# Two weight conversions on ScalarE ordered behind named exps of the attention, in a fused attention and mixture-of-experts kernel

## The chip, the cores and the metric

The kernel runs on one core of one Trainium2 chip. The metric is the device time of one execution in microseconds (us). The engines are called PE (TensorE, matrix products), DVE (VectorE), ACT (ScalarE), POOL (GpSimd) and SP (SyncE, which here only issues transfers). PEld is PE's loading of the stationary operand.

## What is computed

Three stages follow each other. Clustered attention over 2 x 8 heads of 768 rows of 64: a query sees only the keys whose nearest of 16 centroids is its own. Then a layer of 8 experts (512 to 1024 to 512), where each of the 1536 rows goes to the one expert with the largest gate value. Then a dense layer (512 to 2048 to 512) with the activation h * tanh(softplus(h)).

```python
def reference(**kwargs):
    attn_out = _attn_ref(q, k, v, centroids)     # softmax over the keys of the same cluster
    x = attn_out.transpose(0, 2, 1, 3).reshape(B * S, H * D)
    x = _moe_ref(x, modality_id, w_gate, modality_bias, w1, w2)
    return _moe2_ref(x, w_in, w_out)
# _moe_ref, for each expert e:
    h = np.maximum(x[mask] @ w1[e], 0.0)
    out[mask] = gate_w[mask, None] * (h @ w2[e])
```

## The kernel before, in words

All products are made of float16 pairs: a float32 value is split into a high half (hi) and the rest (lo), and a product is the sum of three matmuls, hi*hi, hi*lo and lo*hi.

*Attention* walks over 16 heads with 6 key tiles of 128 each. `st_step` (L382) makes the scores of one key tile in two halves of 384 columns (PE, L391) and their exps (ACT, L393) into the float32 tile `e32` (called `ef` where the exp is used unsplit). `e_hi` (L396) copies it to the hi half `eh` (ACT, L400), `e_low` (L402) makes the lo half `el` on POOL by subtraction (L114), and `av_step` multiplies with the values (L425 to L429). Beside this run, for later heads: `split_pair` (the split `hl` of a pair of heads, L245 on ACT, L249 on POOL), `stack` (SP copies `hl` into the operand tile `QK`, L258 to L261), `assign` (the cluster of each row, ending in a copy `oT` on ACT, L301, that SP loads into `QK`, L303), and `smax` (the row maxima, PE L350 and L355, DVE L351 and L356).

*The gate and the sorting.* When the eight heads of the first batch are done, `gate` ranks its 768 rows by expert and POOL scatters them to DRAM in that order (tensor `dr`, L822). SP brings them back as `xs` (L853), ACT makes a diagonal matrix of each row's gate value (`diag`, tile `dg`, L707), and PE transposes and scales the rows with it (L718) to the sorted block `xw`, which ACT (L722) and DVE (L725) split again.

*The experts.* `moe1` (L948) takes the two experts of a batch with the most rows. It streams their weights in chunks of 512 KB through three helpers: `w_load` (L917) issues the load into the float32 tile `wf`, which has two buffers; `w_hi` (L936) makes the hi half on ACT (L939), `w_lo` (L942) the lo half on DVE (L943), both into tile `w`, which has three buffers. For the first batch the loads are issued by ACT (`WQ = 2`), behind the lo half of the chunk that held the buffer. The first two chunks are loaded and converted ahead of the loop in `moe1`, chunk n + 2 while chunk n is multiplied. The products start when the block `xw` is whole (L1028, read by ACT at L986).

*The dense layer's weights* are turned from float64 to float16 pairs in the meantime: `convs` loads 16 chunks of w_in (tile `raw`, SP, L1040), which DVE shifts and joins (L1048 to L1051, L1056) and ACT copies (L1054).

*Order of the work.* The Python code interleaves these generators; a scheduler then sets the order of the instructions of each engine, except that of SP, which stays as written. An engine takes its instructions in that order, and a waiting instruction holds up all behind it. `moe1` is started when the first weights' loads are issued, while the attention of the second batch goes on:

```python
    wq = []
    for k_ in range(2):
        wq.append(w_hi(wf_t[order[k_]]))
        yield 0.5
        w_lo(wf_t[order[k_]], wq[-1])
        if k_ == 0:
            w_load(*order[2])
        yield 0.5
```

Of the kernel before, what the change touches and what calls it, by code (L numbers as in the profile page):

```python
# [13 lines left out]
AF = mybir.ActivationFunctionType  # L14
# [10 lines left out]
def clustered_attention_moe_kernel(  # L25
# [16 lines left out]
    nc = tc.nc  # L42
    B, H, D, S = qT.shape
# [6 lines left out]
    HS = S // 2  # L50
# [25 lines left out]
    F32T = (2, 5)  # L76
    F32H = 16
    WL = 0
    FAST = 1
    CI1 = 2  # L80
    CQ = 0
# [28 lines left out]
    def eps(shape, dt=F32):  # L110
        return ps_e.tile(shape, dt, tag="e", name="eps")
# [266 lines left out]
        nc.scalar.activation(out=QK[i % NST][96:98, QB, :], in_=pt[96:98, 0:S], func=AF.Copy)  # L378

    e_t = {}  # L380

    def st_step(i, kt):  # L382
        st = QK[i % NST]
        full = i < F32H and kt in F32T
        e32 = a3.tile([P, S], F32, tag="e32", name="ef" if full else "e32", bufs=4)
        eh = None if full else a3.tile([P, S], F16, tag="eh", name="eh", bufs=3)
        el = None if full else a3.tile([P, S], F16, tag="el", name="el", bufs=3)
        sps = [eps([P, 512]) if i < SE and (2 * (T * i + kt) + hf) % SM == SM - 1 else ps_s.tile([P, 512], F32, tag="s", name="s") for hf in range(2)]
        for hf in range(2):
            for a in range(2):  # L390
                nc.tensor.matmul(sps[hf][:, 0:HS], lhsT=st[:, KA + a, kt * P:(kt + 1) * P], rhs=st[:, QA + a, hf * HS:(hf + 1) * HS], start=(a == 0), stop=(a == 1))  # L391
        for hf in range(2):
            nc.scalar.activation(out=e32[:, hf * HS:(hf + 1) * HS], in_=sps[hf][:, 0:HS], func=AF.Exp, scale=1.0 / float(D) ** 0.5)  # L393
        e_t[i, kt] = (eh, el, e32)

    def e_hi(i, kt):  # L396
# [34 lines left out]
    def fin(i):  # L431

        b, h = divmod(i, H)
        av = av_t.pop(i)
        if h == 0:
            xb[b] = l2.tile([P, T, ROW], F16, tag="xb", name="xb")
        x = xb[b]
        r = sm.tile([P, T, 1], F32, tag="r", name="r")
        xt = sm.tile([P, T, D], F32, tag="xt", name="xt", bufs=1)
        nc.vector.tensor_scalar(out=r, in0=av[:, :, D:], scalar1=32.0 / 256, scalar2=32e-9 / 256, op0=ALU.mult, op1=ALU.add)  # L440
        nc.vector.reciprocal(out=r, in_=r)
        nc.vector.tensor_tensor(out=xt, in0=av[:, :, 0:D], in1=r.to_broadcast([P, T, D]), op=ALU.mult)  # L442
        yield 3
        hi = x[:, :, h * D:(h + 1) * D]
        nc.scalar.activation(out=hi, in_=xt, func=AF.Copy)
        yield 2
        (nc.vector if FLD and h == H - 1 else nc.gpsimd).tensor_tensor(out=x[:, :, DM + h * D:DM + (h + 1) * D], in0=xt, in1=hi, op=ALU.subtract)
        fin_done.add(i)
        yield
# [44 lines left out]
    def attention():  # L494
# [28 lines left out]
        def run(g):  # L523
            for _ in g:
                pass
# [10 lines left out]
        def av_next():  # L536

            k = 1 + (len(avq) > AVL)
            while avq and k:
# [9 lines left out]
                if j == 1 and kt == T - 1:  # L549
                    gap[0] = GAP  # L550
                    if i % H == H - 1 and FAST:
                        run(fin(i))
# [57 lines left out]
        for n in range(N + LAG):  # L610
            i, kt = divmod(n, T)
            i_, k_ = divmod(n - LAG, T)
            if n < N:
                if kt == 0:
                    if i + 3 < NH:
                        stack(i + 3)
                    if i == 1:
                        put(gate_consts())
                    if i % H == H - 4 and i < NH - H:
                        load_v(i // H + 1, 0, T)  # L620
                if i % 2 == 1 and kt in (1, 2) and i + 5 < NH:
                    load_pair((i + 5) // 2, kt - 1)
                p_ = i // 2 + 2
                if 2 * p_ < NH:
                    if i % 2 == 0 and kt in (SPK, SPK + 1):
                        run(split_pair(p_, kt - SPK, False, kt - SPK < HLD))
                st_step(i, kt)
# [287 lines left out]
    wf_t = {}  # L915

    def w_load(b, s, n):  # L917

        eng = nc.scalar if WQ and (b, s) == (0, 0) and n < 2 or WQ > 1 and b < WQ - 1 else nc.sync
        if (b, s, eng) not in reg_t:  # L920
            reg_t[b, s, eng] = eng.value_load(reg_t[b][0:1, s:s + 1], min_val=0, max_val=E - 1)
        wf_t[b, s, n] = w_dma(reg_t[b, s, eng], n, eng)
# [13 lines left out]
    def w_hi(f):  # L936
        shp = f.shape
        hl_ = wts.tile([shp[0], 2, shp[1], shp[2]], F16, tag="w", name="w")
        nc.scalar.activation(out=hl_[:, 0], in_=f, func=AF.Copy, scale=32.0)  # L939
        return hl_  # L940

    def w_lo(f, hl_):  # L942
        nc.vector.scalar_tensor_tensor(out=hl_[:, 1], in0=f, scalar=32.0, in1=hl_[:, 0], op0=ALU.mult, op1=ALU.subtract)  # L943
# [4 lines left out]
    def moe1():  # L948

        order = [(b, s, n) for b in range(B) for s in range(2) for n in range(8)]  # L950
# [4 lines left out]
        yield 0.5  # L955
        wq = []
        for k_ in range(2):
            wq.append(w_hi(wf_t[order[k_]]))
            yield 0.5
            w_lo(wf_t[order[k_]], wq[-1])  # L960
            if k_ == 0:
                w_load(*order[2])
            yield 0.5
# [334 lines left out]
    m_p["raw"] = ctx.enter_context(tc.tile_pool(name="raw", bufs=RAWB))  # L1298
    gs0, gs1 = Stepper(lambda: gate(0)), Stepper(lambda: gate(1))
    M = moe1()  # L1300
    CI = convs("i")
    m_done = [0.0]
# [12 lines left out]
    for na, _ in enumerate(attention()):  # L1315
# [6 lines left out]
        if 0 in reg_t and (0, 0, 0) not in wf_t:  # L1322
            wl += 1
            if wl > WL:
                w_load(0, 0, 0)
# [67 lines left out]
```

## Time and profile before

| | us |
|---|---|
| three runs | 675.71, 677.24, 678.28 |
| median | 677.24 |
| profiled execution | 677.5 |
| its span, first to last instruction | 675.8 |

Busy in that span: PE 617.2 us (91%), ACT 455.1 (67%), DVE 375.9 (56%), POOL 256.3 (38%). Attention takes the time to about 300 us, the experts overlap it from 200 on, and the dense layer fills the rest. The shares are averages over stages with different limits, so a change in one stage is read from that stage's own rows. Times in the rows are counted from the span's start; a row gives the start, the duration, and in brackets the idle time of that engine just before it with what ended it.

### The profile page before, as it was taken

The numbers are of one execution on the slowest core, as the hardware profiler recorded it, in microseconds if no ns is written. First come the engines' busy times: TensorE is split into PE (matmuls) and PEld (weight loads), VectorE is DVE, ScalarE is ACT, GpSimd is POOL, SyncE is SP. The second block draws the span as 40 slices with busy tenths as digits, with TensorE's granted clock in tenths as the row PEclk, the third lists the DMA queues.
The fourth block names the chain that finished last, engine by engine and source line by source line (L and its number), as shares of the span: only waits on it lengthen the run. The fifth ranks groups of instructions, "written<-read, shape, count | busy, mean of one in ns | idle before, by whom it ended". The sixth has DMA issues, their size and how long they took to land. (4 is left out here: it accounts for less than half of the span.)

```text
span 675.8 us, 13675 instructions
## 1 busy us (share of the span) xinstructions
PE 617.2 (91%) x5474; PEld 421.9 (62%) x5475; DVE 375.9 (56%) x745; ACT 455.1 (67%) x704; POOL 256.3 (38%) x229
## 2 busy tenths in 40 slices
PE   1789989989698997989999899999999999999995
PEld 1467768858476765656775567566666667666442
DVE  5757666787689899998568898522311101101000
ACT  4578798877697767565887776656655676767300
POOL 5457775887764435220521211111311222223111
PEclk9789999999799999999999999999999999999998
DMA  7632353312971443463454555221000000000000
GB/s 219 156 74 72 90 161 100 94 42 66 274 239 37 135 129 117 144 205 98 168 164 169 157 156 186 63 63 32 32 1 1 17 17 1 31 1 16 17 32 35
DMA packets 56742, 64.42 MB, mean 95 GB/s; under 512 B 10080, under 2 KB 46944, under 8 KB 56672
## 3 DMA queue, kind: packets, MB, share of 16 engines
q1 hardware_dynamic: 42064, 48.74, 25.1%
q10 hardware_dynamic: 12688, 8.42, 4.3%
q0 software_dynamic: 1920, 6.32, 2.5%
q8 instruction: 45, 0.74, 0.5%
q14 instruction: 25, 0.20, 0.1%
HBM read 46.23 MB, written 6.32 MB: 78 GB/s over the span
## 5 line engine op out<-in xcount | busy, mean ns | idle before, releaser
L114 POOL TENSOR_TENSOR el<-e,eh 128x768 f16<-128x768 f32 x64 | 109.0, 1707 | 79.8 <-ACT eh L400 47.8
L1028 PE MATMUL h<-x,win 128*128 128x256 f16 x1152 | 131.8, 273 | 0.2 <-POOL x L1015 0.2
L1028 PEld LDWEIGHTS <-win 128*128 128x128 f16 x1152 | 112.6, 98 | 19.0 <-issue 0.4
L1028 PEld LDWEIGHTS <-w 128*128 128x128 f16 x768 | 74.4, 98 | 66.8 <-issue 11.1
L1133 DVE SCALAR_TENSOR_TENSOR s<-s,h 128x512 f32<-128x512 f32 x48 | 30.8, 684 | 149.0 <-ACT s L1129 149.0
L1184 PE MATMUL o<-wout,xb 128*128 128x512 f16 x432 | 95.9, 379 | 0.0
L114 POOL TENSOR_TENSOR xb<-s,xb 128x1024 f16<-128x1024 f32 x18 | 40.2, 2232 | 134.1 <-ACT xb L1136 134.1
L391 PE MATMUL s<-QK 128*128 128x384 f16 x320 | 78.2, 334 | 7.7 <-ACT e L393 5.9
L1028 PE MATMUL eps<-xw,w 128*128 128x416 f16 x384 | 72.8, 339 | 8.1 <-DVE hT L990 2.9
L351 DVE TENSOR_REDUCE mxh<-x 128x1 f32<-128x512 f32 x96 | 64.7, 681 | 16.3 <-PE x L350 15.8
L1028 PE MATMUL eps<-hT,w 128*128 128x416 f16 x384 | 71.8, 339 | 1.6 <-DVE hT L990 1.6
L1184 PEld LDWEIGHTS <-xb 128*128 128x128 f16 x432 | 42.3, 98 | 48.3
L393 ACT ACTIVATE e<-s 128x384 f32<-128x384 f32 x112 | 52.7, 491 | 22.2 <-PE s L391 18.0
L400 ACT ACTIVATE eh<-e 128x768 f16<-128x768 f32 x64 | 54.2, 849 | 0.7
L391 PEld LDWEIGHTS <-QK 128*128 128x128 f16 x384 | 34.5, 103 | 24.8 <-issue 13.0
L425 PE MATMUL av<-vst,ef 128*128 128x65 f32 x384 | 49.9, 272 | 0.0
L425 PEld LDWEIGHTS av<-vst,ef 128*128 128x128 f32 x384 | 48.5, 191 | 1.9
L427 PE MATMUL av<-vst,eh 128*128 128x65 f16 x384 | 45.4, 193 | 3.1 <-DVE xt L442 2.6
L1127 ACT ACTIVATE s<-h,cst 128x512 f32<-128x512 f32 x48 | 33.0, 688 | 21.7 <-PE h L1028 21.4
L428 PE MATMUL av<-vst,eh 128*128 128x64 f16 x384 | 45.6, 195 | 0.0
L943 DVE SCALAR_TENSOR_TENSOR w<-wf,w 128x1024 f16<-128x1024 f32 x32 | 42.7, 1334 | 4.4 <-ACT w L939 4.3
L429 PE MATMUL av<-vst,el 128*128 128x65 f16 x384 | 43.6, 192 | 0.9 <-POOL el L114 0.8
(245 smaller groups left out, 1090.8 us busy)
## 6 DMA issues: line engine op xcount, KB each, us to landing
wf<-in_moe_w_dram ACTq DMA_DIRECT2D x16, 512.0 KB
raw<-in_moe_w_in_dram SPq DMA_DIRECT2D x16, 512.0 KB
raw<-in_moe_w_out_dram SPq DMA_DIRECT2D x16, 512.0 KB
wf<-in_moe_w_dram SPq DMA_DIRECT2D x16, 512.0 KB
QK<-hl SPq DMA_DIRECT2D x32, 192.0 KB
xs<-dr SPq DMA_DIRECT2D x12, 258.0 KB
t<-in_k_dram SPq DMA_DIRECT2D x8, 384.0 KB
t<-in_q_dram SPq DMA_DIRECT2D x8, 384.0 KB
```

Source lines behind the costliest of these rows:

```text
L114: nc.gpsimd.tensor_tensor(out=out_, in0=in0, in1=in1, op=ALU.subtract)
L351: nc.vector.reduce_max(out=mx_t[i][:, t, 0:1], in_=sp, axis=AX.X)
L391: nc.tensor.matmul(sps[hf][:, 0:HS], lhsT=st[:, KA + a, kt * P:(kt + 1) * P], rhs=st[:, QA + a, hf * HS:(hf + 1) * HS], start=(a == 0), st ...
L393: nc.scalar.activation(out=e32[:, hf * HS:(hf + 1) * HS], in_=sps[hf][:, 0:HS], func=AF.Exp, scale=1.0 / float(D) ** 0.5)
L400: nc.scalar.activation(out=eh, in_=e32, func=AF.Copy)
L425: nc.tensor.matmul(av[:, t, :], lhsT=e32[:, cols], rhs=vs[:, h, :], start=(kt == 0 and t == 0), stop=(kt == T - 1), skip_group_check=True)
L427: nc.tensor.matmul(av[:, t, :], lhsT=eh[:, cols], rhs=vs[:, h, 0:NV], start=(kt == 0 and t == 0), stop=False, skip_group_check=True)
L428: nc.tensor.matmul(av[:, t, 0:D], lhsT=eh[:, cols], rhs=vs[:, h, NV:], start=False, stop=False, skip_group_check=True)
L429: nc.tensor.matmul(av[:, t, :], lhsT=el[:, cols], rhs=vs[:, h, 0:NV], start=False, stop=(kt == T - 1), skip_group_check=True)
L943: nc.vector.scalar_tensor_tensor(out=hl_[:, 1], in0=f, scalar=32.0, in1=hl_[:, 0], op0=ALU.mult, op1=ALU.subtract)
L1028: nc.tensor.matmul(out_, lhsT=wc[:, a, kk, ms], rhs=mv[:, c, kk, :], start=(i == 0), stop=(i == n - 1))
L1184: nc.tensor.matmul(pts[t], lhsT=gsl[q % 2][f // FB][:, f % FB, a, t * P:(t + 1) * P], rhs=wout[:, c, f, :], start=(f == 0 and i_ == 0), st ...
```

## The change

Each exp of the attention is now noted in a list, `e_ins`. The hi half of each of the first two weight chunks is made inside `tc.issue_after(...)` of the twelfth last exp noted so far (`EW = 12`): the scheduler may place the conversion on ACT only behind that exp. Both are ACT's own instructions, so this sets their order and adds no instruction. By the buffer numbers the first conversion (tile `w_3903`) is tied to the first exp of tile `e32_3502`, the second (`w_3951`) to the first exp of `e32_3568`.

```diff
+    EW = 12
...
     e_t = {}
+    e_ins = []
...
         for hf in range(2):
-            nc.scalar.activation(out=e32[:, hf * HS:(hf + 1) * HS], in_=sps[hf][:, 0:HS], func=AF.Exp, scale=1.0 / float(D) ** 0.5)
+            ei_ = nc.scalar.activation(out=e32[:, hf * HS:(hf + 1) * HS], in_=sps[hf][:, 0:HS], func=AF.Exp, scale=1.0 / float(D) ** 0.5)
+            e_ins.append(ei_)
...
         for k_ in range(2):
-            wq.append(w_hi(wf_t[order[k_]]))
+            with tc.issue_after(e_ins[-EW].ins):
+                wq.append(w_hi(wf_t[order[k_]]))
```

The new lines shift the numbers behind them: L393, L400, L707, L722, L933 and L939 of before are L395, L403, L710, L725, L936 and L942 of the change.

The order of ACT's instructions behind the first two weight loads, before. `w` is the converted chunk, `wf` the loaded one, `s` a half of the scores; the rows with DMA issue loads:

```order
L939 ACTIVATE w_3903<-wf_2832 128x1024
L301 ACTIVATE oT_3176<-oC_3314 128x384
L393 ACTIVATE e32_3237<-s_3240 128x384
L939 ACTIVATE w_3951<-wf_2834 128x1024
L393 ACTIVATE e32_3237<-s_3241 128x384
L393 ACTIVATE e32_3276<-s_3279 128x384
L933 ISA
L933 DMA wf_3929<-in_moe_w1_dram 128x4x256
L400 ACTIVATE eh_3238<-e32_3237 128x768
L393 ACTIVATE e32_3276<-s_3280 128x384
L393 ACTIVATE ef_3318<-s_3319 128x384
L400 ACTIVATE eh_3277<-e32_3276 128x768
```

The same place on ACT with the change:

```order
L302 ACTIVATE oT_3176<-oC_3314 128x384
L395 ACTIVATE e32_3237<-s_3240 128x384
L395 ACTIVATE e32_3237<-s_3241 128x384
L403 ACTIVATE eh_3238<-e32_3237 128x768
L395 ACTIVATE e32_3276<-s_3279 128x384
L395 ACTIVATE e32_3276<-s_3280 128x384
L403 ACTIVATE eh_3277<-e32_3276 128x768
L395 ACTIVATE ef_3318<-s_3319 128x384
L395 ACTIVATE ef_3318<-s_3320 128x384
L246 ACTIVATE hl_3273<-t32_3018 128x768
```

Both conversions and the third load are gone from here; exps, their hi halves and the split of the next pair follow each other.

The place on ACT where the two conversions and the third load now stand, with the change; `dg` are the diagonal matrices, `xw` the copies of the sorted block:

```order
L710 ACTIVATE dg_3618<-ident16_103,xs_3482 128x128 x2
L395 ACTIVATE e32_3502<-s_3505 128x384
L942 ACTIVATE w_3903<-wf_2832 128x1024
L302 ACTIVATE oT_3433<-oC_3633 128x384
L725 ACTIVATE xw_3535<-eps_3585 128x4x128
L710 ACTIVATE dg_3668<-ident16_103,xs_3482 128x128 x2
L395 ACTIVATE e32_3502<-s_3506 128x384
L395 ACTIVATE e32_3568<-s_3571 128x384
L942 ACTIVATE w_3951<-wf_2834 128x1024
L403 ACTIVATE eh_3503<-e32_3502 128x768
L936 ISA
L936 DMA wf_3929<-in_moe_w1_dram 128x4x256
```

Before, the conversions of three chunks and the issue of the third to fifth load stood ahead of the first `dg` row; with the change all of these stand behind it, and the conversion of the first chunk comes behind that of the third `dg`.

## Rows read from the trace of the kernel before

**Rows 1.** The cores: span and mean granted clock of PE.

```profile
core 0: 675.8 us, clock 0.985
```

**Rows 2.** Busy us by stretch: its length, PE, PEld, DVE, ACT, POOL, clock, DMA.

```profile
185.00:205.00 20.00, 19.46 (x279) 15.63 (x276) 17.37 (x37) 19.65 (x46) 12.64 (x10) 1.00 0.70 217
...
190.00:220.00 30.00, 26.41 (x334) 20.07 (x333) 27.51 (x57) 25.50 (x57) 16.37 (x14) 1.00 0.39 107
220.00:260.00 40.00, 37.90 (x397) 26.34 (x395) 37.22 (x62) 28.57 (x51) 14.95 (x11) 1.00 0.46 137
260.00:320.00 60.00, 54.95 (x505) 36.71 (x505) 54.37 (x88) 37.26 (x66) 16.48 (x10) 1.00 0.47 141
...
440.00:640.00 200.00, 200.00 (x1319) 128.78 (x1317) 33.19 (x50) 124.81 (x137) 44.32 (x28) 1.00 0.06 19
```

**Rows 3.** The timeline of ACT (ACTq: its issuing of loads), 167 to 180.

```profile
167.89 1.01 ACTq L933 DMA_DIRECT2D wf<-in_moe_w_dram  x2
...
171.62 1.06 ACT L939 ACTIVATE w<-wf 128x1024 f16<-128x1024 f32 x1
172.56 0.85 ACT L301 ACTIVATE oT<-oC 128x384 f16<-128x384 f16 x1
...
178.39 1.06 ACT L939 ACTIVATE w<-wf 128x1024 f16<-128x1024 f32 x1 [4.59 <-issue]
178.68 0.42 ACTq L933 DMA_DIRECT2D wf<-in_moe_w_dram  x1
```

**Rows 4.** The timeline of PE, 172 to 181.

```profile
172.99 0.49 PE L391 MATMUL s<-QK 128*128 128x384 f16 x2
...
174.93 0.49 PE L391 MATMUL s<-QK 128*128 128x384 f16 x2
179.88 1.44 PE L391 MATMUL s<-QK 128*128 128x384 f16 x4 [4.47 <-ACT e L393]
```

**Rows 5.** Busy time by stretch again, around PE's gap.

```profile
177.00:180.00 3.00, 0.12 (x1) 0.10 (x1) 1.23 (x3) 1.61 (x3) 0.93 (x1) 0.52 1.05 399
180.00:184.00 4.00, 4.00 (x32) 2.33 (x30) 3.03 (x6) 3.91 (x7) 2.86 (x2) 0.50 0.79 225
```

**Rows 6.** The timeline of POOL: the lo halves behind the last scatter.

```profile
181.03 3.40 POOL L114 TENSOR_TENSOR el<-e,eh 128x768 f16<-128x768 f32 x2 [3.10 <-ACT eh L400]
```

**Rows 7.** The timeline of SP's issues, 178 to 188.

```profile
178.39 1.23 SPq L303 DMA_DIRECT2D QK<-oT  x2
...
184.04 2.71 SPq L853 DMA_DIRECT2D xs<-dr  x6
```

**Rows 8.** Packets, MB, share by queue in 174-180; 180-184 (two); 184-186; 186-191.

```profile
q1 hardware_dynamic: 523, 0.63, 43.6%
...
q10 hardware_dynamic: 507, 0.50, 40.6%
q0 software_dynamic: 105, 0.32, 31.0%
...
q10 hardware_dynamic: 410, 0.42, 67.4%
...
q1 hardware_dynamic: 859, 1.58, 90.7%
```

**Rows 9.** The timeline of DVE, 173 to 202.

```profile
173.97 0.69 DVE L356 TENSOR_REDUCE mxh<-x 128x2 f32<-128x512 f32 x1 [2.20 <-PE s L391]
...
179.48 1.23 DVE L943 SCALAR_TENSOR_TENSOR w<-wf,w 128x1024 f16<-128x1024 f32 x1 [1.77 <-ACT w L939]
...
201.06 0.48 DVE L1048 TENSOR_SCALAR f<-raw 128x512 int32<-128x512 int32 x1 [0.66 <-DMA raw<-in_moe_w_in_dram]
```

**Rows 10.** The timeline of ACT, 183 to 221.

```profile
183.45 0.38 ACTq L933 DMA_DIRECT2D wf<-in_moe_w_dram  x1
...
191.96 1.27 ACT L707 ACTIVATE dg<-ident,xs 128x128 f16<-128x128 f16 x4
...
220.40 0.52 ACT L986 ACTIVATE hT<-eps 128x416 f16<-128x416 f32 x1 [0.90 <-PE eps L1028]
```

The queues are q1 for what SP issues, q10 for ACT's loads and q0 for POOL's scatters.

## The prediction

> **What bounds the kernel now.** I read the cores first: one core, a span of 675.8 us, mean granted clock 0.985 [rows 1]. The profiled execution took 677.5 us, so 1.7 us lie around the span; that is 0.26 above the median of the three runs, 677.24. Then the table by stretch: from 440 to 640 TensorE (PE) is busy in 200 of 200 us, while VectorE (DVE) and ScalarE (ACT) have room there [rows 2]. So whatever attention delivers earlier, PE keeps to the end. From 190 to 320 DVE is the fullest engine with PE close behind: 27.5 of 30, 37.2 of 40, 54.4 of 60 us [rows 2].
>
> The change touches one place, so I went to ACT's timeline at 167 to 180 [rows 3]. ACT issues the first two weight loads at 167.89. It converts the first chunk at 171.62 without a wait, does one copy (oT) and one exp, and then stands idle for 4.59 us, until 178.39, before the second conversion. Nothing but the landing of that chunk fits: SyncE's queue, whose next descriptor also waits for that load, goes on at 178.39 too [rows 7]. Behind the conversion in ACT's order stands the second half of an exp whose matmul had ended at 172.99 + 0.49 = 173.48 [rows 4]. PE, whose score banks only that exp frees, sits for 4.47 us until 179.88 [rows 4]. In the stretches around it the granted clock falls to 0.52 (177 to 180) and stays at 0.50 until 184 [rows 5], the lower of the two levels, 1.2 GHz, after PE had done almost nothing since 175.4.
>
> **The change, part by part.**
> No instruction is added, and SyncE's order is the same row for row. The two conversions now stand 28 and 31 rows later on ACT, behind the first exps of two later score tiles. By then, past 189 in the working below, chunk 2 has lain there since 178.4. *Removed:* the idle 4.59 us.
>
> *What takes its place on ACT.* From 171.62 on the order is oT, then exps, splits and copies. Successive ACT rows start about 0.1 before the last one ends, so a pair of exps costs 0.86, an eh 0.76. The oT starts at 171.62 instead of 172.56, the first exp ends at 172.86. I follow ACT from there and count where its producer is late:
> 1. the second exp needs the matmul that ends at 173.48: 0.6;
> 2. the fourth needs scores that PE, held by the reduction ending at 173.97 + 0.69 = 174.66 [rows 9], makes at 174.93 + 0.49 = 175.42 [rows 4]; ACT is there at 175.1: 0.3;
> 3. the sixth stands behind two more such reductions: 0.3;
> 4. the two hl splits overwrite the tile that the last `stack` loads from. SyncE's queue still moves 0.63 MB between 174 and 180 [rows 8], and I put the end of those loads at 178.5, an estimate. ACT is there at 177.75: 0.75;
> 5. the xT copy needs transposes that stand on PE behind a reduction matmul on rows loaded at 178.39 [rows 7], landing about 181: 0.25.
>
> Together 2.2 us. ACT then reaches the diagonal copies (dg) at 185.6, with 13.98 us elapsed and 11.8 of work. From 185 to 205 ACT was full before, 19.65 of 20 us [rows 2]. It gets two conversions of 1.06 more there [rows 3], but exactly those left the stretch ahead, so the lead is the difference of the idle: 4.6 - 2.2 = **2.4 us**.
>
> *GpSimd (POOL).* Its scatters end in both orders at 177.93; it then waited 3.10 us, until 181.03, for an eh [rows 6], which now is ready. Its lead is 3.1, more than 2.4, so it does not bind.
>
> *The sorted rows (xs).* The dg copies move ahead of the conversions, so they ask for xs at 185.6 instead of 191.96 [rows 10]. Before, xs was issued at 184.04, when the scatter had landed [rows 7], and its queue brought nothing until 186: the scatter's last 0.32 MB shared 180 to 184 with 0.50 MB of the third weight load, and the fourth load took 184 to 186 [rows 8]. In the new order both loads are issued behind dg. At the 1.58 MB in 5 us of the xs loads themselves [rows 8], 0.32 MB take 1.0 us, so xs is issued near 182; with the 2 us to its first bytes and 0.8 for its first 258 KB it lands near 184.8, ahead of the 185.6. I take no wait, and keep the case that xs comes as before as a rival. The bounds of the new waits are so 0 and 3.4 (2.2 and 1.2 for xs), and those of the lead 4.6 and 1.2.
>
> *Weight loads three to five* are issued by ACT, each behind the lo half that frees its buffer. The third and fourth move from 178.68 and 183.45 [rows 3, 10] to about 195 and 198, the fifth to about 203. The first expert product is read at 220.40 [rows 10]: some 15 us of cover, so I cost it at nothing. If the cover went, the first expert matmuls would wait.
>
> *DVE.* Two lo halves of 1.23 us move with their conversions to 191 to 195; the second of them stood at 179.48, with 1.77 us idle before it [rows 9]. From 190 to 260 DVE has 2.5 + 2.8 = 5.3 us of idle time [rows 2]. It must take in 2.4 of moved work and 2.4 of lead, 4.8: that just fits, and it caps the lead at 2.9 by 260 unless conversions of w_in slip into the 5.6 us that are idle from 260 to 320 [rows 2].
>
> Sum: 677.5 - 4.6 + 2.2 = 675.1; set to the median, which lies 0.26 lower, **674.8 us**.
>
> **Clock.** The rows show 4.0 us of PE work at 0.50 behind the gap [rows 5]. At full clock it would be 2.0 us. In the new order PE has pauses under 1 us there, so I expect 1.00 throughout; but ACT, not PE, was full on the way to 205 [rows 2], so my sum gives nothing for it. The Trainium skill (TensorE: Matmul & The Clock Gate, "HAM oscillation — how this bites in real kernels") says that a long wait for a transfer leaves the matmuls behind it cold at half rate, so that the loss is the wait and half of the cold time. By that rule the sum would be that of the first rival, and the granted clock of this trace agrees with its mechanism.
>
> **The rivals.**
> *The whole stall comes back, with the cold clock.* If PE, not ACT, sets the pace from 180 to 205, the gain is 4.47 idle and 2.0 of half clock: 677.5 - 6.5 - 0.26 = 670.7. For it: PE also counts as busy in 19.5 of 20 us from 185 to 205 [rows 2]. Against it: ACT is as full, and DVE caps the lead at 2.9. Chance 0.2.
>
> *A wait of dg for xs takes the place of the weight wait.* If xs lands as before, from 186 on at 0.8 us a block, dg waits from 185.6 to 186.8: 1.2 us, and the lead is 1.2: 676.0 on the median's scale. With DVE's room used up as well it goes to nothing, 677.2. It decides if xs is issued later than 183. Chance 0.2.
>
> *Slower: the late weight loads meet the w_in loads.* SyncE issues two w_in chunks near 195, just when loads three to five now come: 2.6 MB in all, 8.1 us at the 0.32 MB/us above, so until about 203.6. DVE, which waited 0.66 us for such a chunk before [rows 9], comes to the first chunk's shift near 200 and could then stand 3.6 us there, in front of the sorted block's masks and the reductions. With the 2.4 of moved lo halves finding no idle time either, the change is 677.2 - 2.4 + 3.6 + 2.4 = 680.8. It decides if the first w_in chunk lands after about 200 and pulls the expert's start back. Against it: in the new order that shift stands further back, behind three more of the block's corrections. Chance 0.1. A rule of the Trainium skill speaks for this rival: DMA: Bandwidth & Descriptors, "Rules for kernel authors", says to issue a transfer early and wait late; the change waits late for two chunks and issues three later. No row of this trace shows such a collision yet.
>
> That the change does not do what it says is excluded by the order: both conversions stand where the diff puts them.
>
> **How the numbers follow.** Forecast (lead 1.2 to 4.6) 0.5, by itself 672.6 to 676.0; first rival 0.2, second 0.2, third 0.1. The range takes in the first two rivals with about a microsecond of room above no change and leaves out the third: 670.7 to 678.4. A measurement of this kernel can tell about 0.5%, 3.4 us. Faster by more: the first rival and two fifths of the forecast, 0.40. Slower: the third, 0.10. The rest, 0.50, lies within.
>
> **What would show it.** Right: no ACT idle time before the first two conversions; no PE gap over 1 us at 175 to 180 and a granted clock near 1.00 from 177 to 184; xs issued near 182; the first expert product read near 218 instead of 220.40. Wrong: idle time before dg released by the xs load (second rival), DVE's w_in shift waiting over 2 us for its load (third), or a lead over 4 at the first expert product (first). A lead there that the end doesn't show would say that a later stage gives it back.

## The result: slower by 0.55%, and the profile after

The changed kernel takes 680.81 us (median of 20 executions, 676.44 to 684.78), the kernel before 676.62 us (20 executions, 673.2 to 680.83). The ratio is 1.0055, with a 95% interval of 1.0037 to 1.0073; a later comparison gave 1.0048 (1.002 to 1.0076). The forecast of 674.8 and its range, 670.7 to 678.4, both missed.

The profiled execution of the changed kernel took 677.51 us, near the lower end of its 20, so its trace shows a mild case. Its span, 675.8 us, is that of before only because its first scatter on POOL comes 0.87 us earlier (168.70 against 169.57). Its busy time by stretch, in the columns of [rows 2]:

```profile
185.00:205.00 20.00, 18.14 (x241) 14.60 (x241) 17.77 (x39) 18.55 (x41) 9.95 (x9) 1.00 0.61 180
...
220.00:260.00 40.00, 34.70 (x334) 23.09 (x331) 35.91 (x57) 25.63 (x47) 15.38 (x11) 0.99 0.41 123
```

PE is full from 440 to 640 as before (200 of 200 us). From 220 to 260 it does 34.70 us of work where [rows 2] have 37.90.

Where [rows 3] and [rows 10] stood, ACT's timeline now has:

```profile
174.16 0.49 ACT L395 ACTIVATE e<-s 128x384 f32<-128x384 f32 x1 [2.10 <-PE x L351]
...
177.57 0.87 ACT L395 ACTIVATE e<-s 128x384 f32<-128x384 f32 x2 [2.05 <-remote]
...
186.71 0.68 ACT L710 ACTIVATE dg<-ident,xs 128x128 f16<-128x128 f16 x2
...
190.19 1.07 ACT L942 ACTIVATE w<-wf 128x1024 f16<-128x1024 f32 x1
...
193.69 1.09 ACT L942 ACTIVATE w<-wf 128x1024 f16<-128x1024 f32 x1
193.70 0.39 ACTq L936 DMA_DIRECT2D wf<-in_moe_w_dram  x1
...
216.92 0.50 ACT L990 ACTIVATE hT<-eps 128x416 f16<-128x416 f32 x1
```

The first load of w_in on SP, and DVE's shift of it:

```profile
194.59 1.14 SPq L1044 DMA_DIRECT2D raw<-in_moe_w_in_dram  x2
```

```profile
200.89 0.48 DVE L1052 TENSOR_SCALAR f<-raw 128x512 int32<-128x512 int32 x1 [0.59 <-DMA raw<-in_moe_w_in_dram]
```

The wait for the chunk is gone, neither conversion waits, and the first expert product is read 3.5 us earlier (216.92 against 220.40). That looks like a confirmation. But second profiles of both kernels (runs e15 and e16 below) have it at 218.90 before and 219.62 with the change, two waits of 2.10 and 2.05 stand where one of 4.59 stood, PE does less behind the early product, and the end is not earlier.

A second profile of the same program (run e16) shows a harder case. First its ACT, SP, DVE and PE timelines, then busy time by stretch:

```profile
179.05 1.58 ACT L246 ACTIVATE hl<-t 128x768 f16<-128x768 f32 x2 [3.16 <-DMA QK<-hl]
...
195.05 0.39 ACTq L936 DMA_DIRECT2D wf<-in_moe_w_dram  x1
```

```profile
181.05 2.71 SPq L856 DMA_DIRECT2D xs<-dr  x6
...
195.94 1.14 SPq L1044 DMA_DIRECT2D raw<-in_moe_w_in_dram  x2
```

```profile
203.42 0.43 DVE L1052 TENSOR_SCALAR f<-raw 128x512 int32<-128x512 int32 x1 [2.18 <-DMA raw<-in_moe_w_in_dram]
```

```profile
204.77 0.38 PE L351 MATMUL x<-QK 128*128 128x512 f16 x1 [2.60 <-DVE mxh L352]
```

```profile
200.00:205.00 5.00, 2.40 (x44) 1.94 (x43) 2.82 (x8) 4.91 (x8) 2.52 (x2) 1.00 0.70 232
205.00:210.00 5.00, 5.00 (x41) 3.83 (x40) 5.00 (x9) 0.71 (x2) 1.64 (x1) 0.66 0.01 4
```

A weight load goes out at 195.05, the first two w_in chunks at 195.94. The first of them lands only at 203.42; DVE stands 2.18 us for it, PE 2.60 us for the reductions behind that, and the granted clock is 0.66 in the next 5 us.

### The profile page after: what moved, and what is told of

The parts are those of the page before. It is cut to its first block, busy times and chain, and to the rows that moved or that the text cites. A ratio compares the mean times of both kernels' runs of the same rounds, so it can differ in the third digit from the quotient of the medians.

```text
span 675.8 us, 13680 instructions
## 1 busy us (share of the span) xinstructions
PE 617.8 (91%) x5474; PEld 423.9 (63%) x5475; DVE 374.6 (55%) x745; ACT 453.7 (67%) x704; POOL 253.8 (38%) x229
## 5 line engine op out<-in xcount | busy, mean ns | idle before, releaser
L115 POOL TENSOR_TENSOR el<-e,eh 128x768 f16<-128x768 f32 x64 | 107.6, 1686 | 85.3 <-ACT eh L403 39.1
L393 PE MATMUL s<-QK 128*128 128x384 f16 x320 | 77.9, 333 | 4.1 <-ACT e L395 2.6
L395 ACT ACTIVATE e<-s 128x384 f32<-128x384 f32 x112 | 52.4, 492 | 27.3 <-PE s L393 17.4
L403 ACT ACTIVATE eh<-e 128x768 f16<-128x768 f32 x64 | 54.4, 851 | 0.6
L946 DVE SCALAR_TENSOR_TENSOR w<-wf,w 128x1024 f16<-128x1024 f32 x32 | 47.0, 1468 | 4.6 <-ACT w L942 4.6
L393 PEld LDWEIGHTS <-QK 128*128 128x128 f16 x384 | 33.8, 102 | 21.1 <-issue 9.3
L430 PEld LDWEIGHTS <-eh 128*128 128x128 f16 x384 | 36.8, 99 | 13.8 <-DVE xt L445 8.1
```

The source lines that it names most:

```text
L115: nc.gpsimd.tensor_tensor(out=out_, in0=in0, in1=in1, op=ALU.subtract)
L395: ei_ = nc.scalar.activation(out=e32[:, hf * HS:(hf + 1) * HS], in_=sps[hf][:, 0:HS], func=AF.Exp, scale=1.0 / float(D) ** 0.5)
L403: nc.scalar.activation(out=eh, in_=e32, func=AF.Copy)
L430: nc.tensor.matmul(av[:, t, :], lhsT=eh[:, cols], rhs=vs[:, h, 0:NV], start=(kt == 0 and t == 0), stop=False, skip_group_check=True)
```

## The experiments

The change does two things: it holds two conversions, and the scheduler then orders everything else anew. To part them, most kernels below fix the order of PE, DVE, ACT and POOL by a table taken from the kernel before (or, where said, from the changed one), leaving out only the weight chunks' own instructions. Each entry of the table adds an edge of order, without a wait:

```diff
+ORDER = ...
+    for names in ORDER:
+        for a_, b_ in zip(names, names[1:]):
+            tc.add_manual_dep(traced[b_], a_, mybir.DependencyInfo(mybir.DependencyClass.NoSync, mybir.DependencyReason.DATA), reason="order")
```

In runs e1 and e6, whose table is that of before, the traces have ACT, DVE and POOL in the order of before from 170 to 220, row for row, but for the chunks' own instructions and two that e6 adds. Beside the ratio, I give for most runs the *stretch*: from its first scatter on POOL to the twelfth head's copy `xb` on ACT, in its one profile. In the first profile of before that is 169.57 to 218.97, 49.40 us, in the second (e15) 47.87, so one profile's stretch is uncertain by some 1.5 us. Within one order, what a run loses there is about what it loses in all. From the first scatter to the end of the span it is 506.2 and 504.8 us in the two profiles of before, and in its order 508.5 in e1, 505.6 in e13 and 509.6 in e14. In the order of the changed kernel it is 505.5 in e2, and 507.1 and 509.6 in the changed kernel itself.

**Run e1: the hold alone.** The edit is the change and the table of before. **Run e2: the order alone.** No hold; the table of the changed kernel.

> The change, but every instruction of PE, DVE, POOL and ScalarE other than the first weight chunks' own (their loads, the high and low halves of the first three or four) is kept in the order that it has in the kernel before: the hold alone, without what the scheduler does to the rest. Theory 1 (the lead of some 2.5 us is real; the new order of DVE's queue, which puts the end of a head behind conversions of w_in, loses it in a PE wait of 4 us near 258 and a cold clock behind it): the wait near 258 is gone, and the time is 0.3 to 0.6% under the kernel before (ratio 0.994 to 0.997). Theory 2 (DVE has no room between 190 and 320, whatever the order, so that no lead reaches the end): ratio 0.998 to 1.002. Theory 3 (the weight loads, now later, collide with the loads of w_in, and DVE stands at the first shift of w_in): this stays with the hold, so the kernel is slower than before, ratio 1.003 to 1.008, with 2 us or more of DVE waiting for raw.

> The other half: the two conversions stay where the kernel before has them, without the hold, and the rest of PE, DVE, POOL and ScalarE is put in the order that it has in the changed kernel. Theory 1: the cost lies in the order, so this kernel pays the wait of PE near 258 and does not get the lead: ratio to before 1.005 to 1.012. Theory 2: ratio 0.998 to 1.002. Theory 3: the loads go out as early as before, so nothing is lost: ratio 0.998 to 1.002, DVE waits under 1 us for raw.

Measured: e1 1.0062 (1.0036 to 1.0088), stretch 51.09. e2 1.0013 (0.9986 to 1.004). So the cost is in the hold, the new order costs nothing that can be told, and theories 1 and 2 fall. Theory 3 gave e1's ratio, but its sign is missing there: the w_in shift starts at 201.00 without a wait. ACT in e2, which has no hold:

```profile
175.99 1.06 ACT L939 ACTIVATE w<-wf 128x1024 f16<-128x1024 f32 x1 [2.09 <-DMA wf<-in_moe_w_dram]
...
216.41 0.49 ACT L986 ACTIVATE hT<-eps 128x416 f16<-128x416 f32 x1
```

The first expert product comes at 216.41 without the hold: the early product belongs to the order, and it is worth nothing at the end. In e1, where all else is as before, ACT's timeline shows what the hold does:

```profile
174.89 0.49 ACT L395 ACTIVATE e<-s 128x384 f32<-128x384 f32 x1 [2.24 <-issue]
177.68 0.49 ACT L395 ACTIVATE e<-s 128x384 f32<-128x384 f32 x1 [2.29 <-PE s L393]
...
182.81 0.52 ACT L448 ACTIVATE xb<-xt 128x384 f16<-128x384 f32 x1
...
192.74 1.05 ACT L942 ACTIVATE w<-wf 128x1024 f16<-128x1024 f32 x1
...
196.22 1.06 ACT L942 ACTIVATE w<-wf 128x1024 f16<-128x1024 f32 x1
...
198.96 1.08 ACT L942 ACTIVATE w<-wf 128x1024 f16<-128x1024 f32 x1
...
202.61 0.51 ACT L448 ACTIVATE xb<-xt 128x384 f16<-128x384 f32 x1
```

The same two copies `xb` in the first profile of before, and PE in e1:

```profile
184.91 0.52 ACT L445 ACTIVATE xb<-xt 128x384 f16<-128x384 f32 x1
...
201.25 0.57 ACT L445 ACTIVATE xb<-xt 128x384 f16<-128x384 f32 x1
```

```profile
198.77 1.44 PE L393 MATMUL s<-QK 128*128 128x384 f16 x4 [1.69 <-ACT e L395]
```

Two waits of 2.24 and 2.29 us take the place of the one. At the head's copy near 183 e1 is 13.52 us past its first scatter, 1.8 us further than before's first profile (15.34) and 0.3 further than its second (13.84), although it hasn't done two conversions. Then three of them stand among the exps from 192.7 to 200, PE waits 1.69 us for an exp, and at the next copy (202.61) e1 is 1.6 and 3.2 us late.

**Runs e3 and e4: one engine's order.** The change with the table of before for DVE alone (e3), and for PE alone (e4).

> The change with DVE's queue alone kept in the order of the kernel before (but for the low halves of the first three chunks); the scheduler orders PE, ScalarE and POOL around it. Theory 1: DVE's order is what loses the lead, so this is as fast as the hold alone, ratio to before 0.994 to 0.998, and PE's wait for xt near 258 is under 2 us. Theory 2 and theory 3: still slower than before, 1.003 to 1.008. A fourth theory, that the change only draws another order by chance and any new order costs about that: PE's order differs from both kernels here, so the ratio may be anything from 0.995 to 1.01 and goes with no one wait.

> The change with PE's queue alone kept in the order of the kernel before; DVE, ScalarE and POOL are ordered by the scheduler around it. Theory 1 in its narrow form (DVE's order alone): DVE's order is half way back, since it follows PE's, so ratio 0.996 to 1.004; the wait near 258 is there if r, 1/r and xt stand behind conversions of w_in. A variant of theory 1, that PE's order is what costs (expert products run ahead, then PE has nothing left beside the attention's last heads): ratio 0.994 to 0.997. Theory 2: 0.998 to 1.002. Theory 3: 1.003 to 1.008.

Measured: 1.0198 (1.0153 to 1.0243) and 1.0085 (1.0052 to 1.0119). Neither order undoes the loss. Both are above the 1.003 to 1.008 of the theories that blame the hold, e3 far above, so fixing one engine's order among free ones seems to cost something of its own. I have no shown cause for it, and these two runs decide little.

**Run e5: only the second conversion, soon after its landing.** **Run e6: two copies added.** **Run e7: the second conversion on POOL.** **Run e8: loads late.** All have the table of before.

```diff
 # e5: -22 is the first half of the exp that runs while the chunk lands; the first conversion is not held
-            with tc.issue_after(e_ins[-EW].ins):
+            with tc.issue_after(e_ins[-22 if k_ else -EW].ins) if k_ else ExitStack():
                 wq.append(w_hi(wf_t[order[k_]]))
 # e6: no hold of the conversions; held is e_ins[-EW]
             w_lo(wf_t[order[k_]], wq[-1])
+            with tc.issue_after(held.ins):
+                nc.scalar.activation(out=wq[-1][:, 0], in_=wq[-1][:, 0], func=AF.Copy)
 # e7: no hold, for k_ == 1
+                nc.gpsimd.tensor_scalar(out=wq[-1][:, 0], in0=f2_, scalar1=32.0, scalar2=1.0, op0=ALU.mult, op1=ALU.mult)
 # e8: no hold of the conversions
+                with tc.issue_after(e_ins[-EW].ins):
                     w_load(*order[2])
```

> Only the second conversion is held, and less far: behind the first half of the exp that is seven steps further back than the named one, so that it runs on ScalarE soon after its chunk has landed, with two or three exps ahead of it that it used to hold up. The first conversion and all other work keep the order of the kernel before; the next loads go out within a microsecond or two of where they did. Theory W (what the first two runs point to: the 4.6 us in which ScalarE waited for the chunk would have been waits for PE anyway, so the hold gains only what it leaves undone, and pays for it between 190 and 203, where ScalarE is full): the wait for the chunk is gone and other waits of 3 us or more stand between 171 and 184; ratio to before 0.998 to 1.002. Theory S (the wait for the chunk is worth its price, and only the place that the change gives the conversion is bad): a lead of 1.5 us or more at 190 that stays, ratio 0.995 to 0.998. Theory L (the later loads of weights are what costs): nothing is late here, ratio 0.998 to 1.001.

> The kernel before in its own order, with its conversions where they were, and two instructions added on ScalarE behind the two named exps: each copies the high half of the first and second chunk (128x1024) onto itself. Nothing else moves: it is the price of two microseconds of ScalarE in the place that the change chose. Theory W: ScalarE is full there and PE waits for its exps, so 2 us of work cost 2 us or more: 2 to 3 us late at 205, ratio 1.003 to 1.007. Theory L: loads go out as in the kernel before, ratio 0.999 to 1.002. Theory S: 1.002 to 1.005.

> The kernel before in its own order, with the high half of the second chunk converted on GpSimd instead of ScalarE: GpSimd stands idle where the chunk lands (3.1 us before its subtraction). ScalarE waits for nothing there and has a conversion less (1.06 us). Theory S: a lead of 2 to 3 us at 190, ratio 0.995 to 0.998. Theory W: the lead is what ScalarE has less to do, 1 us at most, if GpSimd's subtraction isn't later by as much: ratio 0.998 to 1.001. Theory L: 0.998 to 1.001.

> The kernel before in its own order, both conversions where they were; only the loads of the third and fourth chunk go out late, behind the exps where the hold alone had them (195 and 199), and the third conversion with its low half follows its chunk. Theory L: this is the cost of the change, ratio 1.004 to 1.008, with DVE waiting over 2 us for raw or PE waiting for the first weights. Theory W: only the third conversion (1.05 us) moves into the full stretch: ratio 1.000 to 1.003. Theory S: 1.000 to 1.002.

Measured: e5 1.0009 (0.9984 to 1.0035), e6 1.0023 (0.9993 to 1.0053), e7 1.0027 (1.0001 to 1.0054), e8 0.9989 (0.9965 to 1.0013). Taking the wait away while keeping the work where it was (e5), or next to it on POOL (e7), gains nothing, so theory S falls; e7 is even a little slower than any theory gave. What e5 does not wait for the chunk it waits for `stack`'s transfers: PE stands 2.31 us for `QK<-hl` until 181.87, and from 185 to 190 the granted clock is 0.50. Late loads by themselves cost nothing (e8), so theory L falls as the only cause. e6's ratio is a little under what theory W gave, and doesn't part it from the others, but its profile shows the price directly. ACT in e6:

```profile
175.97 1.06 ACT L942 ACTIVATE w<-wf 128x1024 f16<-128x1024 f32 x1 [2.32 <-DMA wf<-in_moe_w_dram]
...
183.78 0.52 ACT L448 ACTIVATE xb<-xt 128x384 f16<-128x384 f32 x1
...
190.95 1.27 ACT L710 ACTIVATE dg<-ident,xs 128x128 f16<-128x128 f16 x4
...
192.49 1.05 ACT L966 ACTIVATE w<-w 128x1024 f16<-128x1024 f16 x1
...
197.78 1.06 ACT L966 ACTIVATE w<-w 128x1024 f16<-128x1024 f16 x1
...
202.11 0.57 ACT L448 ACTIVATE xb<-xt 128x384 f16<-128x384 f32 x1
```

Between the two copies `xb` lie 18.33 us; in before it is 184.91 to 201.25, 16.34. Two copies of 1.05 us cost 1.99 us: ACT's work there is paid nearly one for one. The part from the first `dg` to the second copy says it more firmly: it took 9.29, 9.26 and 9.27 us in the two profiles of before and in e5, 11.16 in e6 and 11.15 in e14 (below) with two conversions or copies more, and 12.16 in e1 with three. And in e6, which is the kernel before up to 190, ACT waited 2.32 us for the second chunk, not 4.59.

**Runs e9 to e12: relief from the other side.** In e9 DVE writes the diagonal tiles `dg` in place of ACT; e10 adds the late loads of e8, e11 the hold. e12 is the hold with the two conversions on POOL. Table of before throughout.

```diff
 # e9, e10, e11
+                nc.vector.tensor_scalar(out=dg[:, a], in0=ident16, scalar1=sc[:, 1 + a:2 + a], scalar2=None, op0=ALU.mult)
 # e12: behind the subtraction of the fifth last e_low
+            with tc.issue_after(p_ins[-5].ins):
+                nc.gpsimd.tensor_scalar(out=wq[-1][:, 0], in0=f2_, scalar1=32.0, scalar2=1.0, op0=ALU.mult, op1=ALU.mult)
```

> The kernel before in its own order, but the twelve diagonal tiles dg of the first sorting (128x128 each, 4.1 us of ScalarE between 190 and 203) are written by DVE (128x128 of a short type: 0.15 to 0.2 us each by the xT copy of 128x768 in 0.52, so 1.8 to 2.4 us, where DVE has 2.2 us idle between 190 and 205). It is the price of ScalarE in that stretch from the other side. Theory W (ScalarE is full there, and its work costs one for one): 2 to 3.5 us ahead by 202; ratio 0.995 to 0.998 if that reaches the end. Theory G (what is gained at 202 is given back before 310, since DVE and PE are full there): ahead at 202 but level at 310, ratio 0.999 to 1.002. If ScalarE isn't the bound there: no lead at 202.

> The same as the run before, with the loads of the third and fourth chunk late as in the run on late loads (which showed 1.6 us less between 169 and 201 in its profile and a ratio of 0.999). Theory W: both effects add, ratio 0.993 to 0.997. Theory G: 0.998 to 1.002.

> The hold alone (first run) with the diagonal tiles on DVE: ScalarE does three conversions (3.1 us) more and twelve tiles (4.1 us) less in the full stretch. Theory W: the cost of the hold is gone, ratio 0.997 to 1.001. If the hold costs by its late low halves on DVE or its late loads instead: 1.004 to 1.009, since DVE has 2 us more to do.

> The hold alone, but the two held high halves are converted on GpSimd, at about the same time (behind its subtractions of the same heads), where it stands idle for 7 of 15 us; the third stays on ScalarE. Low halves and loads are as late as in the first run. Theory W: two of the three microseconds that the hold pays on ScalarE are gone: ratio 0.998 to 1.002. If the lateness itself costs: 1.004 to 1.008 as in the first run.

Measured: e9 1.0038 (1.0008 to 1.0068), e10 1.0051 (1.0024 to 1.0078), e11 1.0059 (1.0033 to 1.0086), e12 1.0062 (1.0032 to 1.0092). Theory W in its simple form missed all four, and theory G missed e9 and e10; e11 and e12 came out as their alternatives, late low halves or late loads, had it. ACT isn't the only full thing there. Busy time by stretch in e9:

```profile
190.00:195.00 5.00, 4.11 (x68) 3.27 (x66) 5.00 (x15) 2.73 (x5) 1.31 (x1) 1.00 0.78 184
195.00:200.00 5.00, 4.90 (x57) 4.05 (x55) 5.00 (x13) 3.66 (x10) 2.37 (x2) 1.00 0.57 174
200.00:205.00 5.00, 4.20 (x80) 3.40 (x76) 4.91 (x11) 3.86 (x9) 2.87 (x3) 1.00 0.17 57
```

ACT falls to 10.25 of 15 us and DVE rises to 14.91 (before: 14.90 and 12.82): the bound has changed engines. e12 puts the work on POOL, which has room, and at the copy `xb` near 200 it is 31.03 us past its first scatter, between the 30.15 and 31.68 of before. There it runs into the w_in load. Its SP, DVE and PE timelines and the stretch behind:

```profile
194.09 1.14 SPq L1048 DMA_DIRECT2D raw<-in_moe_w_in_dram  x2
```

```profile
200.50 0.68 DVE L1056 TENSOR_SCALAR f<-raw 128x512 int32<-128x512 int32 x1 [2.08 <-DMA raw<-in_moe_w_in_dram]
```

```profile
202.97 1.25 PE L276 MATMUL eps<-CC,QK 96*128 96x16 f16 x24 [2.90 <-DVE xw L730]
```

```profile
205.00:210.00 5.00, 5.00 (x25) 3.80 (x23) 4.19 (x10) 1.12 (x2) 0.40 (x1) 0.51 0.08 25
```

The chunk lands 6.41 us after its issue (194.09 to 200.50), where in before it took 4.07 (196.99 to 201.06). A weight load had gone out at 193.31. PE waits 2.90 us, and from 205 to 210 the granted clock is 0.51. In e10 the same chunk took 7.05 us (196.03 to 203.08), with a weight load at 195.13.

**Runs e13 and e14: the loads behind w_in's.** e13 is e12, e14 is e1, both with the third and fourth load, and the third conversion, held behind later exps.

```diff
+                with tc.issue_after(e_ins[-EW + 5].ins):
                     w_load(*order[2])
...
+                with tc.issue_after(ld4.ins) if idx == 0 else ExitStack():
                     w_load(*order[idx + 3])
```

> The hold with the two high halves on GpSimd (as in the run before that did this), and the loads of the third and fourth chunk issued only behind the second exp of the next two steps (about 204), so behind the landing of the first w_in chunk; the third conversion is held behind its load. Theory P (the hold has two prices, either of which hides the other: two conversions in a stretch where ScalarE is full, and weight loads that run beside the first loads of w_in, which then land in 6.3 to 7 us instead of 4.1): both are gone here, raw lands 4 to 4.5 us from its issue, DVE waits under 0.7 us for it, and the ratio is 0.997 to 1.001. Theory Q (the rest of the hold costs: low halves late on DVE, or what becomes of the clock): 1.003 to 1.008.

> The hold alone on ScalarE, with the loads and the third conversion late as in the run before this one: only two conversions, 2.1 us, in the full stretch, and no loads beside the first loads of w_in. Theory P: ScalarE's price stays (2.0 us by the run with added copies, of which the conversions left undone between 171 and 185 give back at most what they took): ratio 1.001 to 1.004, between the two others. Theory Q: 1.003 to 1.008.

Measured: e13 0.9997 (0.9972 to 1.0022), stretch 48.92; e14 1.0074 (1.0047 to 1.0101), stretch 51.01. With both prices gone the hold is level, as theory P said. With ACT's alone the loss is the whole of it, more than theory P gave and within theory Q's range: in the order of before either price (e12, e14) is enough, and they don't add. POOL and DVE in e13:

```profile
190.46 1.05 POOL L966 TENSOR_SCALAR w<-wf 128x1024 f16<-128x1024 f32 x1
...
196.64 1.04 POOL L966 TENSOR_SCALAR w<-wf 128x1024 f16<-128x1024 f32 x1
```

```profile
199.55 1.40 DVE L1062 TENSOR_SCALAR f<-raw 128x512 int32<-128x512 int32 x1
```

The w_in chunk, issued at 195.30, no longer keeps DVE waiting.

**Runs e15 and e16: both kernels again,** unchanged.

> The kernel before, unchanged, for a second profile. In the five runs so far that have its order up to there, ScalarE waited 2.1 to 2.5 us for the second chunk, in its own first profile 4.59 us. If the 4.59 us is one execution's and not the kernel's: 2.0 to 2.7 us here. If those runs differ from it by their code: 4 us or more. Ratio 0.998 to 1.002.

> The changed kernel, unchanged, for a second profile. Theory P: raw is issued at about 195 beside a weight load and lands over 5.5 us later; no lead over the run with its order and without its hold is left at 216; ratio 1.004 to 1.007.

Measured: e15 0.9987 (0.9964 to 1.001), stretch 47.87; e16 1.0048 (1.002 to 1.0076), stretch 50.23, its rows above: as expected, with 7.48 us from the issue of the w_in chunk to its shift. ACT and DVE of the kernel before in its second profile:

```profile
176.94 1.06 ACT L939 ACTIVATE w<-wf 128x1024 f16<-128x1024 f32 x1 [3.11 <-DMA wf<-in_moe_w_dram]
```

```profile
200.37 0.43 DVE L1048 TENSOR_SCALAR f<-raw 128x512 int32<-128x512 int32 x1 [1.43 <-DMA raw<-in_moe_w_in_dram]
```

The wait is 3.11 us, above the 2.0 to 2.7 that I had expected and well below 4.59. The difference, 1.48 us, arrives: that execution's copy `xb` comes at 183.44 instead of 184.91, with the first scatter at the same place (169.60), and its span is 674.4 instead of 675.8.

**Runs e17 and e18: the same two edits in the order of the changed kernel.** e17 moves the loads as e14 does, e18 moves loads and conversions as e13 does.

> The changed kernel in its own order, with one thing changed: the loads of the third and fourth chunk go out behind the landing of the first w_in chunk (about 201 to 204), and the third conversion follows its chunk. In the second profile of the changed kernel the w_in chunk landed 7.5 us after its issue and PE stood still for half of 200 to 205. Theory P: raw lands 4 to 4.5 us after its issue, and ScalarE has two conversions in the full stretch instead of three: ratio to before 1.000 to 1.004. If only ScalarE's price counts, as in the run with the hold alone and late loads (1.0074): 1.004 to 1.008.

> The same, with the two held high halves on GpSimd as well: both prices of the hold are gone, in the order of the changed kernel. Theory P: as level as the run that does this in the order of the kernel before (0.9997), ratio 0.997 to 1.002. Theory Q (something else in the hold or its order): 1.003 or more.

Measured: e17 1.0045 (1.0017 to 1.0074), e18 1.0041 (1.0022 to 1.0061). Theory P misses both, e17 narrowly. That only ACT's price counts fits e17, but e18, with the conversions on POOL, is as slow. So theory Q, that something else in the hold costs, is left. Stretches in that order are 45.68 (e2, no hold), 47.02 and 50.23 (the changed kernel's two profiles), 47.17 and 46.88. The long case of 50.23 is not seen in these two, yet some 1.2 to 1.5 us over e2 remain. DVE's rows say where. In e2, then in e18, with one row of busy time by stretch of e18:

```profile
200.90 0.88 DVE L1048 TENSOR_SCALAR f<-raw 128x512 int32<-128x512 int32 x1
...
214.56 0.54 DVE L442 TENSOR_TENSOR xt<-av,r 128x384 f32<-128x384 f32 x1
```

```profile
202.89 0.90 DVE L1062 TENSOR_SCALAR f<-raw 128x512 int32<-128x512 int32 x1
...
213.75 1.22 DVE L948 SCALAR_TENSOR_TENSOR w<-wf,w 128x1024 f16<-128x1024 f32 x1
...
217.69 0.54 DVE L447 TENSOR_TENSOR xt<-av,r 128x384 f32<-128x384 f32 x1
```

```profile
210.00:215.00 5.00, 5.00 (x71) 4.34 (x68) 5.00 (x12) 4.86 (x11) 1.66 (x2) 1.00 0.67 164
```

The w_in shift comes 31.37 us after the first scatter in e2, and 30.95 and 31.43 in e17 and e18: up to there both edits have undone the hold's cost, with the conversions on ACT or not. From the shift to the head's `xt` DVE has no idle time in any of the three, and it takes 13.66 us in e2, 15.57 in e17 and 14.80 in e18. Both have one instruction more there, the third chunk's low half of 1.2 us, which e2 had done at 185.03. In the changed kernel's own profiles the shift comes at 32.19 and 35.24, 0.8 and 3.9 us later than in e2 (1.6 of the 3.9 is a later issue of that load), and the part behind it, with the third low half in it as well, takes 14.18 and 14.34. So in this order the loss reads as the late landing of w_in and a third price, the low half on a full DVE. That price is read from rows of single profiles; no run moved the low half alone, so it isn't shown as the other two are.

No version beat the kernel before by more than the comparisons can tell; e8, at 0.9989, is level with it.

## Why the prediction was wrong, step by step

*"Removed: the idle 4.59 us."* Mis-sized, and the first of the steps that failed. The 4.59 us were one execution's. The same wait was 3.11 us in the second profile of before, and 2.09, 2.32, 2.32, 2.53 and 2.34 us in runs e2, e6, e8, e9 and e10, which have that part of the order. Where the chunk lands earlier, a microsecond of it is worth a microsecond (e15). Where the conversion is put elsewhere (e5, e7), it was worth nothing.

*"Together 2.2 us" of new waits.* Mis-sized as well: 2.24 and 2.29 in e1, 2.10 and 2.05 in the changed kernel, and in its second profile 3.16 us at the hl splits alone, which the prediction had put at 0.75. The removed wait lay beside others, for PE and for SP's transfers, that came out when it went. PE's gap, which was to be under 1 us, was 2.08 (until 178.12). Busy time from 170 to 190, in the two profiles of before and then in the two of the changed kernel:

```profile
170.00:190.00 20.00, 14.11 (x152) 10.26 (x153) 13.94 (x31) 14.97 (x26) 15.26 (x12) 0.83 0.94 293
170.00:190.00 20.00, 16.73 (x165) 11.70 (x165) 15.38 (x34) 16.38 (x28) 16.54 (x13) 0.83 1.00 302
170.00:190.00 20.00, 17.01 (x173) 13.16 (x173) 13.07 (x34) 15.72 (x33) 16.26 (x14) 0.91 0.84 260
170.00:190.00 20.00, 16.76 (x156) 12.66 (x156) 11.14 (x27) 13.99 (x28) 15.93 (x14) 0.83 0.74 239
```

ACT was idle there for 5.03 and 3.62 us before, and for 4.28 and 6.01 with the change. The DMA share there, 0.94 and 1.00 before, suggests that the stretch's transfers hold it up and not the order on ACT; no run tested that by itself.

*"Exactly those left the stretch ahead, so the lead is the difference of the idle."* The step that failed in kind. It holds only where ACT uses the time that the conversions leave. It didn't: the conversions had run in time in which ACT waited anyway, and they went to where ACT is full. In the order of before the price there is nearly one for one (e6: 1.99 us for 2.11 of work).

*"Weight loads three to five ... I cost it at nothing."* Right for the experts' matmuls, wrong for w_in. The first w_in chunk took 4.07 and 4.19 us from issue to shift in the two profiles of before, 6.30 (194.59 to 200.89) and 7.48 in those of the changed kernel. The Trainium skill (DMA: Bandwidth & Descriptors, "Issuing engines are not separate DMA queues") says that transfers of all issuing engines run on the same DMA engines and interleave. The rows agree: the weight loads were ACT's, the w_in loads SP's, and beside the one the other landed later.

*DVE "just fits".* Too kind. With 2 us more work (e9) it is full from 190 to 205, and the kernel is slower by 0.4%; in e17 and e18 the third low half finds no idle time on it.

*POOL and xs.* Right. POOL doesn't bind; xs went out at 181.12 and 181.05, and dg waited for it in neither profile, so the second rival falls.

*The clock "1.00 throughout".* Right in the first profile, 1.00 from 177 to 184. In the second it is 0.50 from 180 to 184, behind a wait of PE of 2.81 us for `QK<-hl`, and 0.66 behind the one that ends at 204.77. The first rival, which wanted stall and cold clock back, falls: in these runs a wait that moved took its cold clock along.

*"Whatever attention delivers earlier, PE keeps to the end."* Wrong as a sign to read. The first expert product came earlier by the order alone (216.41 in e2, 220.40 and 218.90 in the two profiles of before), and e2 is level with before.

*The third rival* gave 680.8, and 680.81 was measured. Its mechanism is there: late weight loads meet w_in's, in the second profile DVE stands 2.18 us (3.6 had been worked out) and PE 2.60, in the first DVE only 0.59. The near agreement is partly luck: it isn't the only price, since e14 has no such meeting and loses 0.74%, and in the changed kernel's own order the loss is still 0.45% without it (e17), where the third low half stands on a full DVE. A chance of 0.1 was too low, since the forecast itself said that DVE had almost no room.

## What to carry to other kernels

Before a wait is booked as a gain, see it in several executions, and ask what else its engine would wait for in the same microseconds: here the engine's idle time hardly fell. Work that ran in an engine's waiting time was free here, and moved into a stretch where that engine is full it cost nearly its whole length, so look at the stretch of arrival on every engine and queue that the step uses. Where a scheduler answers an edit with a new order, fix the old order around the edit and run the two halves apart: an early milestone in the new order may have nothing to do with the edit.

## What the runs showed of the hardware that I had not expected

ACT's wait for the landing of the second 512 KB chunk lay anywhere between 2.09 and 4.59 us in seven executions with the same instructions ahead of it. A 512 KB weight load in the other queue, issued 0.8 to 0.9 us ahead of w_in's two loads, went with a landing of the first of them 6.3 to 7.5 us after its issue (both profiles of the changed kernel, e10, e12), against 4.1 to 4.2 in before, and 4.7 where the weight load was 1.8 us ahead (e8). POOL converts a 128x1024 chunk from float32 to float16 in 1.04 to 1.07 us (e7, e13), as fast as ACT (1.05 to 1.08 in e1).
